# A fused attention and feed-forward kernel on one core: all steps in another order, with the transposing loads of v and the loads of q and k issued further ahead

## The chip, the core and the metric

The kernel runs on one core of a Trainium2 chip, alone. The metric is its time on the device in microseconds; the profile is one execution taken by the hardware profiler.

## What is computed

```python
def _attn_ref(q, k, v, tau):                         # q, k, v: (4, 6080, 256) float32, tau = 1.0
    qn = q / (np.linalg.norm(q, axis=1, keepdims=True) + 1e-06)
    kn = k / (np.linalg.norm(k, axis=1, keepdims=True) + 1e-06)
    s = kn.transpose(0, 2, 1) @ qn / tau             # (4, 256, 256)
    s = s - s.max(-1, keepdims=True)
    a = np.exp(s)
    a /= a.sum(-1, keepdims=True) + 1e-09
    return v @ a

def _moe_ref(x, w_in, w_out):                        # x: (24320, 256), w_in: (256, 2048), w_out: (2048, 256)
    h = x @ w_in
    c = np.sqrt(2.0 / np.pi)
    g = 0.5 * h * (1.0 + np.tanh(c * (h + 0.044715 * h * h * h)))
    return g @ w_out                                 # (24320, 256) float32

def reference(...):
    return _moe_ref(_attn_ref(q, k, v, tau).reshape(24320, 256), w_in, w_out)
```

The attention is across channels: its matrix of scores is 256 x 256 for each of the four batches, summed over 6,080 rows.

## The kernel before, in words

**The work of a batch.** The matrix of scores of a batch is built from q and k, which come in chunks (batch 0 in six, the others in eight chunks of six or so rows for each partition). A chunk's `lq` and `lk` load q and k with a cast to bf16 (L98, in buffers of five per tensor); `qsq` and `ksq` square them (L192, L194), `row0` to `row5` add to the matrix on TensorE (L253, two matmuls each), `f1`, `f2`, `f3` fold the squares on VectorE, `sp` sums them on TensorE, and `sa` (L240) adds them to the norms of the batch. When all chunks are in, a chain of small steps makes the softmax: `gc`, `pow` (a power on POOL, L375), `kf` (VectorE, L381), `kr`, `krp`, `S0`, `S1`, `th0`, `th1`, `dn`, `rc0` to `rc3`, `eT`, `rsum`, `rs`. Since `v @ a @ w_in` is `v @ (a @ w_in)`, the batch's matrix is multiplied into w_in: `aw0` to `aw7` on TensorE (L454), `ac0` to `ac7` copy the result out, `SW0` to `SW2` make sums of it.

**The work of a block.** The output is done in 48 blocks of 512 rows, 12 for each batch, the last of a batch with 448. A block needs v transposed. `lv` casts the block of v to bf16 into a buffer in DRAM (L152, five of them), and `lt` loads it from there with a transposing DMA (L162) into `vT`, of which there are four buffers; the first three blocks of batch 0 are transposed by TensorE instead. The block's first product gives 16 pieces of the hidden layer in eight pairs. A pair is done plainly by `g0` to `g7` (four matmuls of 512 columns, L521) with its GELU in `G0` to `G7` on ScalarE (L531), or two pairs together as a set `w0`, `w1`, `w2`, with seven small products in place of eight: `m1` to `m7` (two matmuls of 256 columns each, L602), copies `cq` and `y5` on ScalarE, sums `ap` (L623) and `ax` (L626) on VectorE, and GELUs `Gq`, `Gr`, `Gx` on ScalarE (L628, L633, L636). The sets need differences of vT, which `vs` makes on VectorE (`sums_v`, L558, L560, L561). Blocks have two or three sets (set 0 alone in block 2, none in blocks 0 and 1). The second product is done in the same way with seven in place of eight: `T1a`, `T2`, `T3`, `T4` on VectorE (L692, L704, L706, L708), `M1A` to `M7B` on TensorE (L736, four matmuls of 256 columns each), `cq`, `y5`, `ap`, `ax`, and four 32 x 32 transposes `c11`, `c12`, `c21`, `c22` on VectorE (L761). The fourth of them issues the block's store, four DMAs on SP's queue (L828).

**The order.** Up to the first product of block 0 the kernel issues its instructions in the order of the code. From there on the order is written out by hand in `ORDER`, a list of 48 strings. String n holds steps in the order in which they are issued, each with the number of the block that it belongs to as a distance from n: in string 3, `M3A-2` is a step of block 1 and `lt+2` the load for block 5. For the steps on q and k, number n stands for chunk n % 12 - 1 of batch n // 12 + 1. There is no scheduler behind it: every engine and every queue gets its instructions in this order and goes through them one by one; semaphores hold an instruction until its inputs are there and its buffer is free. Stores and transposing loads share SP's queue. `lv`, `lq` and `lk` are issued by POOL, whose queue has `pow` in it too, and each waits, as a gate, for the last matmul of the first product (`g` or `m`) ahead of it in the list:

```python
GATE[0] = mm                                   # in mm1 (g); small (m) does the same
...
elif what == "lt":
    load_vt(n)                                 # nc.sync.dma_start_transpose, no gate
elif what == "lv":
    cast_v(n, GATE[0])
elif what in ("lq", "lk"):
    load_one(b, c, "qk".index(what[1]), GATE[0])
```

## Time and profile before

| | |
|---|---|
| time, median of 3 runs | 710.44 us (710.06 to 710.8) |
| the profiled execution's own time | 711.88 us |
| its span, first to last instruction | 709.7 us |
| mean granted TensorE clock | 0.995 |
| busy: TensorE, its weight loads | 681.2 us (96%), 543.6 us (77%) |
| busy: VectorE, ScalarE, POOL | 637.1 us (90%), 625.7 us (88%), 73.4 us (10%) |
| HBM read, written | 78.91 MB, 36.57 MB |

Times in the profile are counted from the first instruction. PE is TensorE, PEld its weight loads, DVE VectorE, ACT ScalarE, POOL GpSimd, SP the engine that issues stores and transposing loads; a q behind a name is that engine's sequencer or queue. A matmul's end is modelled, and a few per cent of the matmuls have no record, so a busy TensorE is not one at its peak. Where an engine was idle ahead of an instruction, the idle time and what ended it stand in brackets, or behind the arrow. The granted clock is the share of the full TensorE clock. The first 38 us are the start (first chunks of q and k, softmax of batch 0); the part that `ORDER` writes out runs from there to the end.

### The profile page before, as it was taken

The numbers are of one execution on the slowest core, as the hardware profiler recorded it, in microseconds if no ns is written. First come the engines' busy times: TensorE is split into PE (matmuls) and PEld (weight loads), VectorE is DVE, ScalarE is ACT, GpSimd is POOL, SyncE is SP. The second block draws the span as 40 slices with busy tenths as digits, with TensorE's granted clock in tenths as the row PEclk, the third lists the DMA queues.
The fourth block names the chain that finished last, engine by engine and source line by source line (L and its number), as shares of the span: only waits on it lengthen the run. The fifth ranks groups of instructions, "written<-read, shape, count | busy, mean of one in ns | idle before, by whom it ended". The sixth has DMA issues, their size and how long they took to land.

```text
span 709.7 us, 14649 instructions
## 1 busy us (share of the span) xinstructions
PE 681.2 (96%) x5634; PEld 543.6 (77%) x5699; DVE 637.1 (90%) x1121; ACT 625.7 (88%) x947; POOL 73.4 (10%) x135
## 2 busy tenths in 40 slices
PE   3999899999999999999999999989999999999996
...
GB/s 242 207 261 198 91 138 127 82 127 197 115 108 91 86 91 141 108 147 133 106 94 115 98 107 116 110 70 86 39 98 90 101 74 57 78 90 59 60 61 56
DMA packets 161462, 79.08 MB, mean 111 GB/s; under 512 B 148448, under 2 KB 152160, under 8 KB 160672
## 3 DMA queue, kind: packets, MB, share of 16 engines
...
HBM read 78.91 MB, written 36.57 MB: 163 GB/s over the span
## 4 chain that ended last, share of the span: by engine, by line
PE 77%; DMA 8%; ACT 8%; DVE 3%; issue 2%; SPq 0%; POOL 0%; DVEq 0%; POOLq 0%; ACTq 0%
PE rp L736 34%; PE h L521 14%; PE rb L602 13%; PE qp L602 10%; PE G L253 4%; DMA vT<-vb 3%; DMA last<-in_k_dram 2%; PE awp L454 2%; ACT g L628 1%; DMA qk_f<-in_q_dram 1%; ACT yw L621 1%; ACT qp L618 1%; DMA win_bf<-in_moe_w_in_dram 1%; ACT g L531 1%; DMA t<-in_k_dram 1%
## 5 line engine op out<-in xcount | busy, mean ns | idle before, releaser
L736 PEld LDWEIGHTS <-wcomb 128*128 128x128 bf16 x2688 | 261.6, 98 | 50.5 <-issue 8.3
L736 PE MATMUL rp<-t,wcomb 128*128 128x256 bf16 (+1 forms) x1504 | 206.6, 272 | 2.2 <-DVE c L752 1.8
L736 PE MATMUL rp<-g,wcomb 128*128 128x256 bf16 (+1 forms) x1128 | 160.5, 272 | 0.5 <-ACT rp L782 0.3
L531 ACT ACTIVATE g<-h 128x1024 bf16<-128x1024 f32 (+1 forms) x136 | 137.2, 1016 | 15.3 <-PE h L521 13.3
L628 ACT ACTIVATE g<-qp 128x1024 bf16<-128x1024 f32 (+1 forms) x124 | 124.7, 1013 | 11.6 <-PE qp L602 9.2
L602 PEld LDWEIGHTS <-sw 128*128 128x128 bf16 x992 | 95.9, 98 | 30.7 <-issue 7.7
L521 PE MATMUL h<-vT,aw 128*128 128x512 bf16 (+1 forms) x403 | 111.9, 376 | 3.0
L623 DVE TENSOR_TENSOR qp<-rb,yw 128x512 f32<-128x512 f32 (+1 forms) x124 | 85.1, 687 | 11.2 <-PE rb L602 6.1
L602 PE MATMUL rb<-tv,sw 128*128 128x256 bf16 (+1 forms) x496 | 93.6, 273 | 0.9 <-ACT qp L618 0.3
L626 DVE TENSOR_TENSOR xw<-rb,yw 128x512 f32<-128x512 f32 (+1 forms) x124 | 83.4, 674 | 6.9 <-PE rb L602 5.0
L602 PEld LDWEIGHTS <-aw 128*128 128x128 bf16 x744 | 72.8, 98 | 13.8
L521 PEld LDWEIGHTS <-aw 128*128 128x128 bf16 x544 | 52.7, 98 | 38.9 <-DVE aw L362 0.6
L636 ACT ACTIVATE g<-xw 128x512 bf16<-128x512 f32 (+1 forms) x124 | 77.3, 625 | 4.4 <-DVE xw L626 4.1
L618 ACT ACTIVATE qp<-rb 128x512 f32<-128x512 f32 (+1 forms) x124 | 71.9, 582 | 5.6 <-PE qp L602 1.5
L633 ACT ACTIVATE g<-rb 128x512 bf16<-128x512 f32 (+1 forms) x124 | 72.7, 593 | 4.1 <-PE rb L602 4.0
L621 ACT ACTIVATE yw<-qp 128x512 f32<-128x512 f32 (+1 forms) x124 | 73.0, 594 | 3.5 <-PE qp L602 1.9
L192 ACT ACTIVATE sq<-t 128x1536 bf16<-128x1536 bf16 (+4 forms) x49 | 64.6, 1335 | 6.0 <-DMA t<-in_q_dram 6.0
L761 DVE STREAM_TRANSPOSE ot<-rp 128x256 f32<-128x256 f32 (+1 forms) x141 | 59.1, 434 | 8.3 <-PE rp L736 6.1
L253 PE MATMUL G<-t 128*128 128x256 bf16 (+1 forms) x352 | 61.0, 280 | 0.1
L708 DVE TENSOR_TENSOR t<-t,g 128x2048 bf16<-128x2048 bf16 (+2 forms) x49 | 57.9, 1184 | 2.0 <-ACT g L633 0.8
L706 DVE TENSOR_TENSOR t<-g 128x2048 bf16<-128x2048 bf16 (+2 forms) x49 | 57.7, 1180 | 0.1
L692 DVE TENSOR_TENSOR t<-g 128x2048 bf16<-128x2048 bf16 (+1 forms) x48 | 57.5, 1198 | 0.1
...
## 6 DMA issues: line engine op xcount, KB each, us to landing
...
vb<-in_v_dram POOLq DMA_DIRECT2D x41, 256.0 KB, 4.6
...
```

Source lines behind the costliest of these rows:

```text
L253: nc.tensor.matmul(G[b][:, jc, :], lhsT=qt[:np_, r, jc * 128 : jc * 128 + 128], rhs=kt[:np_, r, :], start=first and jc == 0, stop=jc == 1, ...
L521: mm = nc.tensor.matmul(hp[:, u, :cols], lhsT=AW[b][:, cc, fc * 128 : fc * 128 + 128], rhs=vt_tiles[n][:, cc, :cols], start=cc == 0, stop= ...
L531: nc.scalar.activation(gs(n)[:, 2 * p : 2 * p + 2, :cols], HP.pop((n, p))[:, :, :cols], AF.Gelu_apprx_tanh)
L602: GATE[0] = nc.tensor.matmul(acc[:, u * hc : u * hc + hc], lhsT=lhs[:, u * 128 : u * 128 + 128], rhs=rhs, start=m in (1, 5) and u == 0, st ...
L618: nc.scalar.activation(qp(n, i)[:, 0, :c], RB[n, i][:, :c], AF.Copy)
L621: nc.scalar.activation(YW[n, i][:, :c], qp(n, i)[:, 1, :c], AF.Copy)
L623: nc.vector.tensor_add(qp(n, i)[:, 1, :c], RB[n, i][:, :c], YW[n, i][:, :c])
L626: nc.vector.tensor_add(XW[n, i][:, :c], RB[n, i][:, :c], YW.pop((n, i))[:, :c])
L628: nc.scalar.activation(gs(n)[:, 2 * pa : 2 * pa + 2, :c].rearrange("p u (t x) -> p t u x", t=2), QP.pop((n, i))[:, :, :c].rearrange("p t ( ...
L633: nc.scalar.activation(gs(n)[:, 2 * pb : 2 * pb + 2, :hc], two(RB.pop((n, i))[:, :c]), AF.Gelu_apprx_tanh)
L636: nc.scalar.activation(gs(n)[:, 2 * pb : 2 * pb + 2, hc:c], two(XW.pop((n, i))[:, :c]), AF.Gelu_apprx_tanh)
L736: nc.tensor.matmul(ACCS[n, acc][:, :hc], lhsT=wcomb[:, w, fc, :], rhs=x, start=first and k == 0, stop=k == 3, skip_group_check=True)
```

## The change

All 48 strings of `ORDER` are replaced, and nothing else in the code. Both lists hold the same 3,897 steps of the same blocks, so the kernel issues the same instructions, with the same shapes, tiles and buffers. What differs is the order on each engine and queue, and with it the matmul on which a gated load waits. Most steps move by a few places; loads and casts move by up to several blocks. By the TensorE steps ahead of them in the list, 26 of the 45 `lt`, 24 of the 48 `lq` and `lk` and 21 of the 45 `lv` stand earlier than before, the others later. Below are the strings of which the text speaks, before and after.

```diff
 ORDER = [
@@ strings 0 to 3 @@
-    """g0 lv+3 aw2 lv+4 ac2 aw4 ac4 lq+1 g1 lk+1 G1 G0 aw3 lq+2 ac3 aw5 ac5 aw6 g3 G3 aw7 g2 ac6 G2
-    ac7 g7 G7 pA11 SW0 vtp vtc0 g6 G6 lv+5 vtc1 pS3 g5 vtq G5 g4 G4 pA12 M1B""",
-    """g3 G3 T1a-1 pF0-1 pS1-1 M1A-1 pF1-1 pS2-1 g0 G0 M5A-1 T2-1 T4-1 M5B-1 y5-1 cq-1 g1 G1 lq+2
-    g2 M2B-1 lq+4 M6B-1 g7 pNA-1 G2 M6A-1 vtr0-1 M2A-1 G7 lk+1 qsq g6 G6 pS4-1 g5 c11-1 ap-1
-    M3B-1 T3-1 vtr1-1 vs+1 G5 M7A-1 M7B-1 ax-1 g4 G4 lk+2""",
-    """w0m1 T1a-1 ksq-1 w0m5 M3A-2 w0cq w0y5 M4A-2 M4B-2 c21-2 g0 G0 c12-2 c22-2 lq+2 w0m6 w0ap
-    M1A-1 M5A-1 M5B-1 ksq lt+1 lv+5 T2-1 f1-1 M1B-1 g3 w0m7 w0ax w0m2 w0m3 y5-1 cq-1 M6B-1 M6A-1
-    G3 g7 T4-1 w0Gq w0m4 G7 w0Gr M2B-1 T3-1 M2A-1 c11-1 ap-1 w0Gx g4 vs+1 G4 g5 T1a G5 M3B-1
-    lk+2 M7A-1 SW2-2 g6 G6 row4-1 SW1-2""",
-    """w0m1 w0m5 w0cq M3A-2 w0y5 f2-2 row3-1 M7B-2 ax-2 w0m6 w0ap g3 ksq M4A-2 lt+1 M4B-2 G3 c21-2
-    row5-2 w0m7 c12-2 c22-2 g0 w0ax qsq M1A-1 G0 w0Gx f3-2 M1B-1 T2-1 T4-1 M5B-1 w0m4 w0Gr M5A-1
-    y5-1 cq-1 T3-1 w1m1 w0m2 w0m3 w0Gq T1a sp-2 sa-2 row1-2 w1m5 w1cq w1y5 M6A-1 M6B-1 g7 G7
-    w1m6 w1ap M2B-1 M2A-1 c11-1 row0-2 row5+1 lt+2 ap-1 qsq-1 f1-1 f2-1 g4 M3B-1 G4 M7B-1 M7A-1
-    ax-1 qsq+1 row5-1 w1m7 w1ax w1m2 w1m3 c22-1 M4B-1 lk+2 M3A-1 M4A-1 row3-2 w1Gx f3-1 sp-1
-    w1Gq vs+1 sa-1""",
+    """g0 lv+3 aw2 ac2 aw5 ac5 aw4 g1 G0 ac4 aw3 ac3 aw7 aw6 ac6 G1 ac7 g3 G3 pS3 g2 G2 pA11 g7 G7
+    vtp vtc0 lv+4 g6 G6 M1B lq+1 g5 G5 lq+2 g4 G4 vtc1 SW1 T1a pF0 M1A pA12 vtq""",
+    """g3 pS1-1 G3 pF1-1 pS2-1 g0 G0 M5A-1 M5B-1 lk g1 g2 lk+1 T2-1 vtr1-1 y5-1 cq-1 M2B-1 M6A-1
+    lq+2 G1 T4-1 g7 lt+2 G2 lt+3 M6B-1 vtr0-1 T1a G7 g6 G6 pNA-1 lq+3 M2A-1 pS4-1 c11-1 ap-1 g5""",
+    """w0m1 g4-1 G5-1 G4-1 M3B-2 T3-2 M7A-2 M7B-2 SW0-2 lk+1 M3A-2 vs w0m5 w0cq ax-2 g5 c12-2 w0y5
+    row1-1 G5 T2-1 w0m6 row3-1 M4A-2 w0ap M4B-2 g0 c21-2 w0m7 M1A-1 M5A-1 qsq-1 ksq w0ax c22-2
+    G0 SW2-2 w0m2 w0m3 w0Gq M1B-1 M5B-1 T3-1 y5-1 cq-1 w0Gx row4-1 w0m4 g3 G3 lk+2 ksq-1 g6 G6
+    M2A-1 M6B-1 f1-1 T4-1 g7 w0Gr lv+3 lv+5 lt+3 G7 M2B-1 M6A-1 g4 G4""",
+    """w0m1 c11-2 ap-2 M3A-2 vs w0m5 M3B-2 c12-2 w0cq T1a-1 g3 w0y5 G3 w0m6 M7A-2 M7B-2 w1m1 w0ap
+    qsq-1 g0 lq+2 G0 ax-2 M4A-2 M4B-2 T2-1 c21-2 c22-2 w0m7 lv+3 w0ax w0m2 w0m3 w0Gq w1m5 w1cq
+    M1B-1 M5A-1 M1A-1 M5B-1 row4-1 w0m4 row0-2 w1m6 f2-2 row5-2 y5-1 cq-1 M6B-1 M2A-1 T3-1 qsq
+    M6A-1 f3-2 w0Gx M2B-1 T4-1 g7 w0Gr vs+1 w1y5 sp-2 row2-2 c11-1 G7 ap-1 M7A-1 lk+3 M7B-1 w1ap
+    w1m2 w1m3 f1-1 w1m7 ax-1 lk+2 g4 qsq+1 f2-1 f3-1 lq+3 M4A-1 G4 M4B-1 sa-2 w1ax T1a sp-1 sa-1
+    w1Gx lt+3 M3A-1 M3B-1 lv+5 c22-1""",
 ...
@@ strings 9 to 10 @@
-    """w0m5 f2-1 w0m1 w0cq w0y5 g0 lt+2 M4A-2 w0m6 row4-1 lq+5 lv+3 G0 w1Gx-1 w0ap M4B-2 c21-2 w1m1
-    w1m5 w1cq w0m7 w1y5 w0ax w0Gx row5-2 w0m3 M1B-1 f3-1 c22-2 w1m6 w1ap gc w0m4 w0Gr M1A-1
-    M5B-1 M5A-1 y5-1 T2-1 lk+6 cq-1 w1m2 w1m3 vs+1 w0m2 w1Gq w0Gq sp-1 sa-1 w1m7 w1ax T3-1 pow
-    M6A-1 M6B-1 M2B-1 w2m1 M2A-1 c11-1 ap-1 w2m5 w1Gx g3 w2y5 w2cq w1m4 w1Gr G3 M3B-1 T4-1 w2m6
-    M3A-1 w2ap kf kr M7A-1 M7B-1 ax-1 w2m3 w2m2 c12-1 w2Gq w2m7 w2ax krp S1+1 th1+1 M4A-1 S0+1
-    th0+1 M4B-1""",
-    """w0m5 c22-2 c21-2 w0m1 w0cq g0 w0m6 T1a-1 M1A-1 M1B-1 w0y5 w0ap lt+2 dn rc1 rc0 G0 w2Gx-1
-    T2-1 M5A-1 M5B-1 y5-1 w0m3 w0m2 g3 w0Gq w2m4-1 w2Gr-1 w0m7 g4 rc2 w1m1 cq-1 M2B-1 rc3 w0ax
-    M6B-1 G3 G4 lq+5 w1m5 M6A-1 lt+3 w1cq eT w1y5 M2A-1 c11-1 w0Gx w1m6 w0m4 w0Gr g7 G7 ap-1
-    M3A-1 w1ap w1m7 w1m2 w1m3 w1Gq M3B-1 T3-1 vs+1 lq+7 rsum+1 rs+1 w1ax T4-1 M7A-1 M7B-1 ax-1
-    w1Gx aw0+1 ac0+1""",
+    """w0m1 w0m5 w1ax-1 w1m4-1 w0cq w0y5 M3A-2 M4A-2 w0m6 T1a-1 f1-1 M4B-2 g0 lk+5 f2-1 w1Gr-1 w0ap
+    w0m3 f3-1 w1Gx-1 c21-2 w0m7 w1m1 c12-2 w0ax G0 T2-1 T4-1 w0m2 w0Gq M1A-1 M1B-1 w1m5 w1cq
+    w0m4 row4-2 w0Gr w1y5 M5A-1 M5B-1 y5-1 cq-1 w1m6 sp-1 w2m5 sa-1 w2y5 w0Gx w1ap T3-1 row2-2
+    row1-2 w2m1 w2cq pow M6A-1 w1m2 w1m3 w1Gq kf w1m7 w1ax gc lq+5 lv+5 M6B-1 M2B-1 c22-2 kr
+    w2m6 w2ap M2A-1 w1Gx g3 G3 c11-1 ap-1 w2m7 w2ax w2Gx krp S0+1 S1+1 th1+1 M7A-1 M7B-1 w2m3
+    w1m4 w1Gr w2m2 w2Gq ax-1 M4B-1 M4A-1 vs+1 c22-1""",
+    """w0m5 w0m1 w0cq w0y5 T1a-1 M3B-2 M3A-2 th0 dn w0m6 c12-2 c21-2 w0ap w2m4-1 g0 T2-1 M1A-1 G0
+    rc1 M1B-1 rc2 w0m3 w0m2 w0Gq w0m7 lq+3 w2Gr-1 T4-1 w0ax M5A-1 T3-1 M5B-1 y5-1 cq-1 rc0 g3 G3
+    g4 G4 w1m1 M2A-1 w1m5 w1cq M6A-1 w1y5 M6B-1 w0m4 w0Gr w0Gx w1m6 w1ap M2B-1 g7 lt+2 lt+3
+    c11-1 ap-1""",
 ...
@@ strings 23 to 24 @@
-    """g3 G3 M7B-2 rc0-1 g0-1 G0-1 ax-2 g7-1 G7-1 c12-2 eT-1 w1ax-1 M4A-2 rsum rs w0m1 T1a-1 w0m5
-    w0cq w0y5 M4B-2 c21-2 w1m4-1 w1Gx-1 aw0 ac0 w0m6 w1Gr-1 g0 lk+5 G0 M1B-1 aw1 ac1 w0ap w0m7
-    w0m3 T2-1 w0m2 w0Gq lv+4 w1m1 w1m5 w1y5 w1cq lt+2 aw2 w0ax w0Gx ac2 T3-1 M1A-1 M5A-1 M5B-1
-    y5-1 cq-1 w1m6 w1ap w0m4 w2m5 w0Gr aw3 ac3 M2B-1 M6A-1 w2m1 w1m7 M6B-1 lv+6 SW0 qsq+2 M2A-1
-    w1ax aw4 w1m3 w2y5 w2cq w2m6 w1Gx lt+3 ac4 w1m2 w1Gq w1m4 w1Gr c11-1 ap-1 M3A-1 M7A-1 w2ap
-    T4-1 M7B-1 aw5 M3B-1 vs+1 w2m3 ac5 c22-2 w2m2 w2Gq""",
-    """w0m5 w0m1 w0cq lv+6 aw6-1 ac6-1 w0y5 w2m7-1 ax-2 M4A-2 M4B-2 T1a-1 w0m6 g3 G3 w2ax-1 w2m4-1
-    c21-2 c12-2 aw7-1 w0ap w0m7 M1B-1 f1+1 ac7-1 w2Gx-1 w0m3 w0m2 g0 w0Gq M5B-1 SW1-1 T2-1 M5A-1
-    G0 M1A-1 w2Gr-1 g7 w0ax vs+1 y5-1 w1m1 cq-1 w1m5 w1cq M6A-1 w1y5 M6B-1 G7 row3+3 w1m6 w0Gx
-    f2+1 w1ap T4-1 w0m4 w0Gr row5+1 M2A-1 M2B-1 lv+4 c11-1 ap-1 w1m3 w1m2 w1Gq g4 T3-1 lt+3 G4
-    row4+2""",
+    """g3 G3 lv+3 g0-1 G0-1 M7A-2 rc0-1 lt+2 M7B-2 g7-1 w0m5 w0Gr-1 G7-1 rc2-1 rc1-1 rc3-1 eT-1
+    ax-2 w1m1 rsum rs lq+6 w0m1 M4A-2 w0cq lv+5 T1a-1 aw0 ac0 M4B-2 w0m6 w0y5 w0ap w1Gx-1 lk+4
+    g0 G0 c12-2 aw1 c21-2 T2-1 ac1 w0m3 w0m2 w0Gq w0m7 M1A-1 M5A-1 aw2 w0ax lv+6 ac2 T3-1 w1m5
+    w1y5 w1cq lt+3 M1B-1 M5B-1 lv+4 aw3 ac3 w2m5 w1m6 w1ap y5-1 cq-1 w0Gx w0m4 w0Gr M2B-1 M6B-1
+    w2y5 w2m1 M6A-1 M2A-1 w2cq lq+5 T1a w2m6 qsq+2 aw4 ac4 w1m3 w1m2 w1m7 w1Gq c11-1 ap-1 M3A-1
+    M7B-1 w2ap w2m3 lv+8 w2m7 w1ax w1m4 M7A-1 w1Gx lk+5 w1Gr w2m2 w2Gq vs+1 aw5 ac5 M3B-1""",
+    """w0m1 SW0-1 w0m5 c22-3 T4-2 w0cq w0y5 ax-2 g3 aw6-1 ac6-1 w2ax-1 w0m6 M4B-2 w0ap M4A-2 f1+1
+    c21-2 aw7-1 c12-2 w0m3 w0m2 ac7-1 w2Gx-1 T2-1 SW1-1 w2m4-1 G3 w0m7 g0 M1A-1 w0Gq w2Gr-1 w0ax
+    T4-1 G0 M1B-1 M5A-1 M5B-1 y5-1 cq-1 w1m1 w1m5 w1cq g7 w1y5 M2B-1 G7 w1m6 w1ap w0m4 w0Gr vs+1
+    M6A-1 M2A-1 M6B-1 c11-1 ap-1 T3-1 w1m3 w1m2 w0Gx w1Gq g4 G4 w1m7 M3A-1""",
 ...
@@ strings 28 to 30 @@
-    """w0m5 w1m4-1 row0-2 row1-1 w1Gr-1 M3B-2 w0m1 w0y5 lk+4 w0cq row2-1 T4-2 row5 T1a-1 M3A-2
-    w2Gr-1 w0m6 w0ap w1Gx-1 M7A-2 w1m1 M7B-2 f3-1 ax-2 ksq+1 w0m7 w0ax w0m3 w0m2 w0Gq g0 G0
-    M4B-2 M4A-2 w2m5 w2y5 lk+3 w0m4 T2-1 w0Gr g3 c21-2 G3 c12-2 row4 row4-1 w2m1 w2cq T4-1 M1B-1
-    M5B-1 w0Gx w1m5 w1y5 T3-1 w2m6 w2ap M1A-1 w1cq M5A-1 lq+2 c22-2 w2m7 w2ax w2m3 w1m6 w1ap
-    y5-1 cq-1 w2m2 M2A-1 M2B-1 c11-1 w2Gx w1m7 w1ax w2Gq lq+3 w1m3 w1m2 w1Gq row4+1 M6B-1 w1m4
-    w1Gr M6A-1 w2m4 vs+1""",
-    """w0m5 w0y5 w0m1 w0cq ap-2 M3A-2 M7A-2 M7B-2 w2Gr-1 w1Gx-1 vs+1 w0m6 w0ap qsq-1 M3B-2 c12-2 g0
-    G0 w0m7 w0m2 w0m3 ax-2 lk+1 w0ax w0Gq T1a-1 M4A-2 M4B-2 c21-2 w0m4 g3 w2m5 w0Gx w0Gr M1A-1
-    M1B-1 M5A-1 M5B-1 qsq T2-1 T3-1 sp-2 sa-2 c22-2 row3+2 row5+2 row0+2 lt+2 w2m1 y5-1 cq-1
-    M6A-1 M2B-1 f1-1 f2-1 f3-1 w2y5 M2A-1 lq+3 w2cq w2m6 w2ap G3 qsq+2 M6B-1 w1m5 c11-1 ap-1
-    w1m1 lv+5 w1cq row2+2 w2m3 w2m2 w2Gq w2m7 w2ax T4-1 M7A-1 M3B-1 w1m6 w1y5 M3A-1 w1ap w2m4""",
-    """g0 w2Gx-1 M7B-2 w2Gr-1 ax-2 G0 w1m7-1 w1ax-1 w1m3-1 w1m2-1 w1Gq-1 sp-2 sa-2 M4B-2 T1a-1
-    M4A-2 w1Gx-1 w1m4-1 g3 w1Gr-1 G3 w0m5 row0 row5 w0y5 w0m1 w0cq c12-2 ksq+1 c21-2 M1A-1 M5A-1
-    w1m5 c22-2 M1B-1 w0m6 T2-1 M5B-1 row0-1 vs+1 row2-2 w0ap w1m1 w0m3 w0m2 T4-1 w0m7 y5-1 cq-1
-    w1cq M6B-1 w1y5 w1m6 row0+2 w0Gq row4+2 M2A-1 w0ax w0Gx w0m4 w1ap w1m7 w0Gr w1m3 w1m2 w1Gq
-    g7 G7 f1-1 w1ax w1m4 w1Gr""",
+    """w0m5 w0y5 row0-1 c11-2 ap-2 T1a-1 row3 M3B-2 w0m1 w0cq f2-1 g0 lq+3 w0m6 M3A-2 row5+1 w2Gr-1
+    M7A-2 ksq+1 G0 w0ap w0m7 w0ax M7B-2 ax-2 w0m3 row2+1 w0m2 w0Gq w0m4 w0Gr M4A-2 M4B-2 T3-1 g3
+    w2m1 c12-2 w0Gx G3 w1m1 w2m5 w2y5 c21-2 c22-2 vs+1 M1B-1 M5B-1 w1m5 M5A-1 row0+1 T2-1 w2cq
+    w2m6 M1A-1 row1-1 w1y5 w1cq w1m6 row4 y5-1 cq-1 w2ap w2m7 w1ap w2m3 qsq w2ax w2Gx M6B-1
+    M6A-1 w1m3 w1m2 w1Gq T4-1 w1m7 w1ax w2m2 w2Gq M2A-1 M2B-1 c11-1 ap-1 w2m4 w1m4 w1Gr row0+2
+    T1a row2""",
+    """w0m5 M3B-2 w0y5 vs+1 w0m1 lt+2 w0cq lv+4 f3-2 M7B-2 w1Gx-1 M3A-2 w0m6 M7A-2 qsq g0 G0 w0ap
+    ax-2 w0m7 w0ax w0m2 M4A-2 w2Gr-1 M4B-2 c12-2 w0m3 w0Gq w0m4 w0Gx w0Gr c21-2 c22-2 g3 G3
+    M1A-1 T2-1 T4-1 M1B-1 lq+3 M5A-1 M5B-1 w1m1 sp-2 sa-2 row4+2 w2m5 w1m5 w2m1 row0+2 y5-1 cq-1
+    M2A-1 M6A-1 T3-1 w2y5 w2cq f1-1 w2m6 w2ap w1cq w1y5 M6B-1 f2-1 qsq+2 lv+6 M2B-1 c11-1 ksq+2
+    row5+2 row3+1 ap-1 w2m7 w2ax w1m6 w1ap w2Gx w2m3 w2m2 w2Gq f3-1 M3B-1 lv+3 M7A-1 M7B-1 w1m7
+    ax-1 w1ax T1a w2m4 w2Gr w1m3 w1m2 w1Gq M4B-1 M4A-1 M3A-1 c12-1 w1m4 w1Gr sp-1 sa-1 lk+3
+    c21-1 f1""",
+    """g3 w0m5 w0m1 M1A-1 M5B-1 w1Gx-1 T3-1 G3 w0y5 w1m1 g0 w0cq w0m6 M1B-1 G0 M5A-1 y5-1 cq-1 T2-1
+    row2+1 w1m5 w1cq w0ap w1y5 w0m7 w0m3 vs+1 w0ax w0Gx w0m2 M2A-1 w1m6 w1ap c22-2 M6B-1 M6A-1
+    f2-1 M2B-1 c11-1 ap-1 w0Gq lt+2 lt+3 w0m4 w0Gr w1m3 w1m2 f3-1 w1Gq g7 G7 M3A-1 T1a w1m7 w1ax
+    ksq""",
 ...
@@ string 33 @@
-    """w0m5 w1m4-1 w1Gx-1 G7-1 sp-1 sa-1 w1Gr-1 g0 row3-3 G0 T3-1 gc M4B-2 M4A-2 c21-2 w1m1 c12-2
-    w0y5 w0m1 w0cq T2-1 g3 G3 pow kf kr M1A-1 M1B-1 w0m6 w0ap M5B-1 M5A-1 w1m5 y5-1 cq-1 vs+1
-    w0m7 w0ax w0m2 w0m3 M6A-1 M6B-1 T4-1 lt+2 w1cq w1m6 w1y5 M2A-1 w0Gq w1ap c22-2 w0m4 M2B-1
-    c11-1 ap-1 w0Gx krp S1+1 S0+1 lt+4 w0Gr T1a w1m3 w1m2 w1Gq g4 G4 M7B-1""",
+    """g0 f1-1 c12-2 w1Gq-1 f2-1 f3-1 M7B-2 sa-2 sp-1 G0 M7A-2 T1a-1 row4-1 w1m1 row1-3 sa-1 ax-2
+    vs+1 pow kf w0m1 w0m5 lt+3 M4B-2 M4A-2 c21-2 w1Gx-1 gc g3 T3-1 w0y5 w0cq w0m6 w0ap M1A-1
+    M5B-1 M5A-1 M1B-1 kr lv+4 G3 T2-1 krp S0+1 y5-1 w1m5 cq-1 w0m7 w1cq w1y5 T4-1 th0+1 w0m2
+    w0m3 w0Gq w0ax M2B-1 M2A-1 w1m6 M6B-1 w0Gx M6A-1 w0m4 w0Gr w1ap w1m7 c22-2 S1+1 th1+1 w1m3
+    w1m2 w1Gq g4 G4 c11-1 ap-1 M3B-1 M3A-1 M7B-1 dn+1""",
 ...
@@ string 47 @@
-    """w0m5 M4A-2 c22-2 M4B-2 w1Gx-1 w2Gq-1 T1a-1 w0y5 w0m1 w0cq M3B-2 c12-2 c21-2 w2Gx-1 g3 T3-1
-    G3 w1m4-1 w2m4-1 w1Gr-1 w0m6 M1B-1 w0ap w2Gr-1 M1A-1 M5B-1 M5A-1 w0m2 y5-1 cq-1 w1m5 T2-1
-    T4-1 w1m1 w1cq w1y5 w0m3 w0Gq w0m7 M6B-1 M6A-1 w0ax w0Gx w1m6 M2A-1 M2B-1 w1ap c11-1 ap-1
-    w2m5 w2m1 w1m7 w1ax w2y5 w1m3 w1m2 w2cq w1Gq w0m4 M7A-1 w2m6 w2ap w1m4 w0Gr M7B-1 g0 G0 w2m7
-    ax-1 M3A-1 M4A-1 M4B-1 w2ax w2Gx T1a w1Gr M3B-1 c12-1 c21-1 c22-1 w1Gx T2b w2m3 w2m2 w2Gq
-    M5A T2a M5B y5 T3a M1B M1A w2m4 cq T3b M3A M6B w2Gr M6A y6 M3B M7A a12 c12 M7B ax c22 sA T4b
-    M4B M2B T4a M2A c11a c11 M4A c21 sB""",
+    """w0m1 w0m5 ax-2 M4A-2 w0y5 w0cq w1Gx-1 T1a-1 M4B-2 w2ax-1 w2Gx-1 c22-2 M3B-2 c12-2 w1m4-1
+    w1Gr-1 w2m4-1 c21-2 w2Gr-1 w0m6 w0ap g3 G3 M1B-1 M1A-1 M5B-1 M5A-1 y5-1 cq-1 w0m7 w1m5 w1m1
+    T2-1 w0m2 w0m3 M6A-1 w1cq w1y5 T4-1 M6B-1 w1m6 M2B-1 w0ax w0Gq w0Gx T3-1 M2A-1 w1ap w2m5
+    w2y5 w2m1 w2cq w0m4 w1m3 w1m2 w1Gq c11-1 ap-1 w1m7 M7A-1 w1ax w2m6 w1Gx M7B-1 w2ap ax-1 w0Gr
+    w1m4 g0 w2m7 M3A-1 w2ax M4A-1 G0 M4B-1 w2Gx T1a M3B-1 w2m3 w2m2 w1Gr w2Gq c21-1 c12-1 c22-1
+    M5A M5B y5 M1A T2b M1B cq T2a w2m4 T3a w2Gr T3b M3A M6B M6A T4b y6 M3B a12 c12 M7A M7B ax
+    c22 T4a M4A M4B c21 M2A M2B sA c11a c11 sB""",
 ]
```

367 lines of the change are left out of this document (184 added, 183 removed).

## The prediction

> **What bounds the kernel now.** I read the page's slices first, then the stretches (busy time of each engine, granted clock, DMA share), then the chain of work that ended last, and last the timeline at the places where the stretches fall off.
>
> ```profile
> span 709.7 us, 14649 instructions
> ...
> PE   3999899999999999999999999989999999999996
> ```
>
> After the start TensorE is in the nineties throughout, but for an 8 in the fifth and one in the 27th slice. In the stretches the columns are PE, PEld, DVE, ACT and POOL busy, granted clock, DMA share, GB/s.
>
> ```profile
> 37.85:705.70 667.85, 655.08 (x5384) 523.15 (x5449) 619.29 (x1091) 608.88 (x930) 56.87 (x104) 0.99 0.61 105
> 40.00:50.00 10.00, 9.95 (x62) 5.16 (x61) 9.30 (x17) 8.06 (x9) 2.37 (x5) 1.00 1.16 278
> 50.00:60.00 10.00, 9.91 (x66) 6.34 (x65) 9.52 (x14) 9.97 (x12) 1.61 (x3) 1.00 1.06 210
> 75.00:100.00 25.00, 23.14 (x193) 18.16 (x193) 23.79 (x49) 20.42 (x29) 1.53 (x3) 1.00 0.57 104
> 100.00:150.00 50.00, 49.62 (x434) 41.08 (x437) 46.74 (x81) 47.72 (x71) 6.80 (x13) 1.00 0.63 107
> 300.00:350.00 50.00, 49.34 (x418) 39.76 (x421) 47.69 (x88) 48.05 (x74) 6.70 (x12) 1.00 0.83 136
> 450.00:460.00 10.00, 9.95 (x88) 8.11 (x87) 8.65 (x15) 9.87 (x14) 0.81 (x2) 1.00 1.12 135
> 464.10:470.90 6.80, 5.97 (x29) 4.11 (x29) 4.73 (x7) 2.25 (x3) 0.00 (x0) 0.50 0.64 120
> ```
>
> An ordinary stretch (100 to 150, 300 to 350) leaves TensorE 0.4 to 0.7 us idle in 50; VectorE and ScalarE follow at 47 and 48. So TensorE is the bound, and the other two have too little slack to make up a stop. Two stretches are not ordinary: 1.86 us idle in 75 to 100, and a clock of 0.50 from 464.1 to 470.9. The chain at the first:
>
> ```profile
> 65.06 0.87 SPq L828
> ...
> 66.04 7.01 DMA vT<-vb
> 73.06 0.02 issue
> 73.08 0.44 DVE tv L558
> ```
>
> The timeline behind it, with the idle time ahead of an instruction and what ended it in brackets:
>
> ```profile
> 77.88 1.03 PE L736 MATMUL rp<-t,wcomb 128*128 128x256 bf16 x8 [1.75 <-DVE c L752]
> ```
>
> The chain at the second, and its timeline:
>
> ```profile
> 450.99 12.11 DMA vT<-vb
> ```
>
> ```profile
> 463.19 0.43 DVE L558 TENSOR_TENSOR tv<-vT 128x512 bf16<-128x512 bf16 x1 [3.33 <-DMA vT<-vb]
> ...
> 464.93 0.58 PE L602 MATMUL qp<-vT,sw 128*128 128x256 bf16 x2 [3.04 <-DVE qp L623]
> ```
>
> Both times a transposing load of v lands at the moment at which VectorE wants it for `sums_v` (L558). VectorE's queue stands behind that instruction, its other results come late, and TensorE stops: 1.75 us before 77.88, 3.04 before 464.93. After the second stop the clock is 0.50 for 6.8 us, which costs 6.8 x 0.5 = 3.4 more. **The two places hold 1.75 + 3.04 + 3.4 = 8.2 us.** The list of waits, over the whole span, has no third (us in total, times, longest):
>
> ```profile
> DVE tv L558 <- DMA vT<-vb: 5.5, 2, 3.3
> ```
>
> **What the change does to the loads of v.** Both orders have the same 3,897 steps, so the sum consists of waits alone. To compare, I lay both orders on TensorE's work, with each step at what TensorE takes for it back to back in the chain:
>
> ```profile
> 449.94 0.44 PE rp L736 x4
> 450.38 0.22 PE rb L602 x2
> ```
>
> ```profile
> 78.91 0.22 PE G L253 x2
> 79.13 0.22 PE rb L602 x2
> 79.35 0.86 PE h L521 x4
> ```
>
> A `g` is 0.86, an `M` 0.44, a small product or a `row` 0.22 (0.863, 0.436 and 0.218 unrounded), an `aw`, two of the four matmuls of a `g`, 0.43. There are 136, 672, 868, 144 and 30 of them; with 7/8 of it in the four short blocks that is 642.6 us with the odd small steps. Counted from 37.85, a load of v can be issued when three things are over: what is ahead of it on SP's queue (a store waits there for its block's fourth transpose, then takes 2.2), the last use of the buffer that it takes over (there are four), and its own cast (6 us after the matmul on which that is gated).
>
> ```profile
> 80.33 2.19 SPq L828 DMA_DIRECT2D out_dram<-ot  x4
> ```
>
> ```profile
> vb<-in_v_dram POOLq DMA_DIRECT2D x41, 256.0 KB, 4.6
> ```
>
> A load's lead is the TensorE work from there to its first use. In the order before, the shortest come out as 4.7 (block 3), 4.8 (14), 8.6 (42), 10.7 (31) and 11.1 (28). The rows above have 4.9 for block 3 (66.04 to 73.08, less its wait, the 5.5 - 3.3 = 2.2 of the list) and 8.9 for block 31 (450.99 to 463.19, less 3.33), so the method is good to some 2 us. Against them, the landing of all 45 loads:
>
> ```profile
> DMA to landing us min/median/max: 3.0/4.2/12.1
> ```
>
> In the order after, the shortest leads are 16.2 (block 32), 17.1 (27), 17.3 (43) and 17.5 (40). Block 3's load moves from string 2, behind the store of block 0, to string 1 with no store ahead of it: its lead goes from 4.7 to 28.2, block 31's from 10.7 to 25.8. Seventeen of the 45 get a shorter lead, but none goes under 16.2, which is 4 us more than the longest landing. So both stops go: -8.2.
>
> **The loads of q and k** go from a shortest lead of 6.5 (q of step 7) to 9.8 (q of step 17); half of the 48 stand later in the order than before, so it is the short ones that grow. Times to landing of those issued from 40 to 44.2 us, then of those from 53 to 61:
>
> ```profile
> DMA to landing us min/median/max: 12.6/13.0/13.5
> ```
>
> ```profile
> DMA to landing us min/median/max: 4.4/6.8/7.3
> ```
>
> The one at risk is k of step 1: its gate lets it go at 50.5, and `row1-1` in string 2 wants it at 61.7, a lead of 11.2. It lies between the two groups, nearer to the later. Taken at 8 to 9 it costs nothing; at 13.5 it costs 2.3.
>
> **What else moves.** `kf` on VectorE needs `pow` on POOL, which needs `sa` on VectorE:
>
> ```profile
> 504.74 0.15 DVE L240 TENSOR_TENSOR sv<-sv,ss 128x4 f32<-128x4 f32 x1
> ...
> 504.97 1.95 POOL L375 TENSOR_TENSOR rt<-sv,halves 128x4 f32<-128x4 f32 x1 [6.04 <-DVE sv L240]
> ```
>
> ```profile
> L375 POOL TENSOR_TENSOR rt<-sv,halves x3: 1027/1049/1952, 170.9 to 505.0; 128x4 f32<-128x4 f32 x3
> ```
>
> Before, 3 to 4.3 us of VectorE's steps lie between `sa` and `kf` in all three batches. After, it is 1.8 in the first, 4.9 in the second and 1.3 (one add and one `sums_v`) in the third. `pow` is over 0.23 + 1.05 or 0.23 + 1.95 us after `sa` starts, so VectorE stands 0 to 0.4 in the first and 0 to 0.9 in the third, with its whole queue behind `kf`. I take 0.3 for both, as two of the three durations are near the short one.
>
> The small waits are left. 667.85 less 642.6 is 25.3; without the 8.2 there remain 17 us, 0.3 or so for each of the 48 blocks. For twelve kinds of pairs (VectorE or ScalarE makes something, a step of TensorE reads it) I counted how often less TensorE work lies between the two than the making takes: 321 of 1,158 pairs before, 293 after. In proportion that would be 1.5 us fewer; VectorE's work is a little more bunched, though (below). I take 0, with a bound of 2 us down and 3 up. The end, where T4 is done in halves with products behind it, keeps one stop in either order: 0, within the same bounds.
>
> **Sum.** The profiled execution took 711.88 (its span and 2.18 around it); less 8.2, plus 0.3, that is 704.0. The median of the timed runs, 710.44, lies 1.44 under it: 710.44 - 7.9 = **702.5 us**. That difference also says that the 6.4 us at 462 are in the timed runs: an execution that had them alone would lie at least that far above the median.
>
> The price of the second stop rests on the clock. The Trainium skill ("TensorE: Matmul & The Clock Gate", section "HAM oscillation — how this bites in real kernels") has it that idle gaps of over about 3.4 us are to be avoided. Here a gap of 3.04 us had half the clock for 6.8 us behind it: the trace is harsher than the rule. By the rule alone that stop would be worth 3.04, and the sum would be 705.9.
>
> **The rivals.**
> *The early loads collide at the start (0.10).* Two transposing loads now run from about 50 us, beside q and k of the first chunks, where the DMA share is 1.16 and 1.06: nothing is to spare. If k of step 1 lands only 13.5 us after its issue, TensorE stands 2.3 us at `row1-1`: 704.8. If the transposing loads add some 3 us each, the stop goes past the 3.04 us at which the clock fell and is worth about 6.4: 708.9. Against it, fewer loads are queued ahead of it. Before, five are issued by 44 us:
>
> ```profile
> 39.18 1.05 POOL L152 DMA_DIRECT2D vb<-in_v_dram  x2 [1.96 <-PE h L521]
> 40.22 0.58 POOL L98 DMA_DIRECT2D t<-in_q_dram  x1
> 41.23 0.54 POOL L98 DMA_DIRECT2D t<-in_k_dram  x1 [0.43 <-PE h L521]
> 43.55 0.53 POOL L98 DMA_DIRECT2D t<-in_q_dram  x1 [1.78 <-DMA wst<-in_moe_w_out_dram]
> ```
>
> After, it is one by 44 and four by 47. The skill has the reason in general ("DMA: Bandwidth & Descriptors", section "Issuing engines are not separate DMA queues"): DMAs of all queues run on the same 16 engines and interleave, so an earlier issue brings no bandwidth.
> *The 12.1 us landing is the profiled execution's own (0.04).* Then only 1.75 goes: 710.44 - 1.75 + 0.3 = 709.0. Against it stands the 1.44 above.
> *The change does not do what it says (0.02),* because SP's queue or the buffers hold the loads as before: 710.4. Against it, the leads above have queue and buffers in them.
> *VectorE's work is bunched and stops TensorE (0.17), slower.* With its steps scaled to what VectorE is busy (619.29), each free to start where it stands in the order, they queue up 6.3 us deep in string 24 after (5.8 in string 10, 5.0 in string 23), where a batch's softmax and its products with w_in come on top; before, those three have 2.7, 3.8 and 3.1. If TensorE then stands as it did at 462, each place costs 6.4. From the second such stop it decides: 702.5 + 2 x 6.4 = 715.3. One alone leaves the kernel faster (708.9). Against it: before has 5.4 in string 1 and 5.3 in string 20, and the stretches that hold them (50 to 60, 300 to 350) do not fall off.
>
> **How the numbers follow.** Forecast 0.67, rivals 0.10, 0.04, 0.02 and 0.17. The range goes down to 700.5 by the 2 us of the small waits, and up to 710.5, which leaves out the slower rival alone. A measurement of this kernel can tell about 0.2% (1.4 us) from no change: faster by more are the forecast and the collision (0.77), within it are the landing of one execution and the idle change (0.06), slower is the bunching (0.17).
>
> **What would show it.** Right: no wait of L558 for vT, no stretch with a clock under 1.00, no 8 in TensorE's slices after the start; at most 1 us of waiting at `kf` near 500. Wrong: a stop of TensorE over 1 us in strings 10 or 23 to 25 that VectorE ends, a wait for `in_k_dram` or `in_q_dram` near 62 us, or another stretch at half the clock.

## The result and the profile after

| | before | after |
|---|---|---|
| median of the timed runs, us | 710.25 (6 runs, 709.07 to 712.25) | 699.41 (6 runs, 699.12 to 705.56) |
| profiled execution, us (span) | 711.88 (709.7) | 705.56 (703.8) |

The ratio is 0.986, with a 95% interval of 0.9825 to 0.9895: the kernel after is faster by 10.8 us. The forecast was 702.5 with a range from 700.5, so the direction was right and the gain was larger than the range allowed for. The profiled execution is the slowest of the six of after; the other five lie 5.3 us and more under it, and its profile shows why. The page, span and TensorE's slices:

```profile
span 703.8 us, 14646 instructions
...
PE   3997999999999999999999999999999999999996
```

The two 8s of before, in the fifth slice and near 462 us, are gone; there is a new 7 in the fourth slice. The stretches (columns as before: PE, PEld, DVE, ACT and POOL busy, granted clock, DMA share, GB/s):

```profile
60.00:65.00 5.00, 2.84 (x23) 2.02 (x21) 3.76 (x11) 4.36 (x6) 0.53 (x1) 1.00 1.03 47
65.00:70.00 5.00, 3.03 (x15) 2.16 (x15) 0.70 (x1) 0.57 (x1) 0.00 (x0) 0.67 1.04 201
75.00:100.00 25.00, 24.84 (x198) 18.96 (x200) 22.87 (x41) 21.54 (x27) 4.70 (x9) 1.00 0.92 161
100.00:150.00 50.00, 49.79 (x437) 41.82 (x440) 47.66 (x83) 48.07 (x75) 7.40 (x15) 1.00 0.78 128
300.00:350.00 50.00, 49.56 (x417) 39.96 (x421) 47.16 (x88) 48.20 (x74) 5.61 (x8) 1.00 0.61 106
460.00:470.00 10.00, 9.93 (x80) 7.65 (x79) 9.35 (x17) 9.51 (x16) 0.50 (x1) 1.00 0.58 93
```

From 75 to 100 TensorE is idle for 0.16 us instead of 1.86, and from 460 to 470 it runs at full clock: both stops of before are gone, and the list of waits has no entry of L558 for vT any more. What is new lies from 60 to 70. The chain of waits, the list of waits and the timeline there:

```profile
52.29 14.64 DMA t<-in_k_dram
66.93 0.04 issue
66.97 0.59 PE G L253 x2
```

```profile
PE G L253 <- DMA t<-in_k_dram: 4.5, 2, 4.1
```

```profile
66.97 0.59 PE L253 MATMUL G<-t 128*128 128x256 bf16 x2 [4.13 <-DMA t<-in_k_dram]
```

k of step 1, the load that the prediction named as the one at risk, took 14.64 us to land, TensorE stood for 4.13 us at `row1-1`, and the clock fell to half behind it. That is the first rival, in this one execution, and one of the signs of being wrong that the prediction names (a wait for `in_k_dram` near 62 us, with half the clock behind it).

To see the rest I lay both orders on TensorE's work as the prediction does, and now subtract that work from the start that each block's first step has in the trace. What is left is the time that TensorE has lost so far, from block 0 on. For the kernels of this document, in us (the experiments follow below):

| lost by block | 2 | 4 | 23 | 30 | 31 | 47 |
|---|---|---|---|---|---|---|
| before | 0.6 | 2.9 | 8.5 | 11.1 | 17.2 | 22.3 |
| after, first profile | 1.2 | 7.3 | 11.2 | 12.2 | 12.4 | 16.6 |
| after, third profile (e15) | 1.0 | 1.2 | 5.2 | 6.2 | 6.4 | 10.6 |
| two loads and k moved (e7) | 0.7 | 0.8 | 6.4 | 9.1 | 9.3 | 14.5 |
| order of before, leads of after (e2) | 0.9 | 1.0 | 6.5 | 9.1 | 9.5 | 14.5 |
| after, k of step 1 earlier (e4) | 0.9 | 1.2 | 5.1 | 6.1 | 6.3 | 10.4 |
| first half of before, second of after (e10) | 0.5 | 0.5 | 6.0 | 7.6 | 7.8 | 11.7 |
| e2 with 27 rows as fill (e12) | 0.7 | 0.8 | 6.3 | 10.4 | 11.0 | 16.0 |

Before loses 2.3 at block 3 and 6.1 at block 30, which are the two stops (8.4), and 13.9 in small waits. After loses 5.9 at block 2, which is the late load, and 10.7 in small waits. So the small waits, which the prediction took to stay, sum to 3.2 us less.

### The profile page after: what moved, and what is told of

Its sections match the earlier page's. It is cut to its first block, busy times and chain, and to the rows that moved or that the text cites. A ratio compares the mean times of both kernels' runs of the same rounds, so it can differ in the third digit from the quotient of the medians.

```text
span 703.8 us, 14646 instructions
## 1 busy us (share of the span) xinstructions
PE 676.3 (96%) x5635; PEld 543.6 (77%) x5699; DVE 636.4 (90%) x1121; ACT 625.2 (89%) x947; POOL 74.2 (11%) x135
## 4 chain that ended last, share of the span: by engine, by line
PE 75%; ACT 9%; DMA 7%; issue 4%; DVE 4%; POOL 0%; DVEq 0%; POOLq 0%; ACTq 0%
PE rp L736 34%; PE rb L602 13%; PE h L521 12%; PE qp L602 10%; PE G L253 5%; DMA t<-in_k_dram 5%; ACT g L628 2%; ACT yw L621 1%; DMA t<-in_q_dram 1%; ACT qp L618 1%; ACT g L531 1%; PE awp L454 1%; DMA out_dram<-ot 1%; ACT sq L192 1%; ACT g L633 1%
## 5 line engine op out<-in xcount | busy, mean ns | idle before, releaser
L253 PE MATMUL G<-t 128*128 128x256 bf16 x352 | 59.7, 278 | 4.5 <-DMA t<-in_k_dram 4.5
L704 DVE TENSOR_TENSOR t<-g,t 128x2048 bf16<-128x2048 bf16 (+2 forms) x49 | 57.4, 1173 | 0.5 <-ACT g L636 0.2
```

The lines of the kernel that those rows point to most:

```text
L253: nc.tensor.matmul(G[b][:, jc, :], lhsT=qt[:np_, r, jc * 128 : jc * 128 + 128], rhs=kt[:np_, r, :], start=first and jc == 0, stop=jc == 1, ...
```

## The experiments

The theory to test (A): the gain is made of two parts, the two stops behind late transposing loads of v, and small waits that hang on the order of the computing steps. Against it stood that the two loads are the whole gain, that the stop at 462 us belonged to the profiled execution, or that the order of the computing steps alone did it. Kernels that are compared with each other in the first four experiments ran on one chip, beside the kernel before (710.19, 17 runs). e5 to e8, e9 to e12 and e13 to e15 ran on three other chips; the kernel before took 710.49, 710.20 and 711.53 there.

**e1: two loads moved in the kernel before.**

```diff
 # string 1
-M3B-1 T3-1 vtr1-1 vs+1
+M3B-1 T3-1 vtr1-1 lt+2 vs+1
 # string 2
-ksq lt+1 lv+5
+ksq lv+5
 # string 28
-M5A-1 lq+2 c22-2 w2m7
+M5A-1 lq+2 c22-2 lt+3 w2m7
 # string 29
-row0+2 lt+2 w2m1
+row0+2 w2m1
```

> The kernel before, with two transposing loads of v moved and nothing else: that of block 3 from string 2 to string 1 (behind `vtr1-1`, with no store ahead of it), that of block 31 from string 29 to string 28 (behind `c22-2`, ahead of the store of block 27). Theory A (the two stops behind late loads are worth 8.2 us in the timed runs, and the rest of the gain, some 3 us, are small waits that hang on the order of the computing steps): 710.25 - 8.2 = 702.0, no wait of L558 for vT at blocks 3 and 31. Rival B (the two loads are the whole of it): 699.4. Rival C (the stop and the half clock at 462 us belong to the profiled execution of before): 708.5, as only the 1.75 us of block 3 go.

Measured: 715.66 us, ratio 1.0075 (1.0053 to 1.0098). Slower than before, which no theory had. The stop at 462 is gone, but at 67 us there is a larger one than either of before. The list of waits, TensorE's timeline, and the stretch:

```profile
DVE sq L194 <- DMA t<-in_k_dram: 14.7, 3, 9.3
```

```profile
75.73 0.61 PE L736 MATMUL rp<-t,wcomb 128*128 128x256 bf16 x2 [9.00 <-DVE t L704]
```

```profile
70.00:80.00 10.00, 4.26 (x17) 2.43 (x18) 5.83 (x6) 0.63 (x1) 0.00 (x0) 0.52 1.07 193
```

VectorE waits 9.3 us for k of step 2 (`ksq` on it, L194), its queue stands behind that, and TensorE stops for 9.00 us, with half the clock after it. Between 51 and 61 us, the loads issued and their median times to landing:

```profile
t<-in_q_dram POOLq DMA_DIRECT2D x2, 384.0 KB, 16.8
t<-in_k_dram POOLq DMA_DIRECT2D x2, 384.0 KB, 16.1
vT<-vb SPq DMA_TRANSPOSE x1, 19.4
```

In the kernel before, the loads of q and k of these microseconds took 4.4 to 7.3 us. The transposing load of block 3, now issued at 49.7, takes 19.4, and the loads of q and k that run beside it are slow as well. What moved was one load; what came late was another one.

**e2: all loads as far ahead as after, the computing steps as before.** The four kinds of load steps of before's order are put at the lead that they have after (or as far as the ring of buffers allows); all other steps keep their order.

> The computing steps in the order of before, and every load of q, k and v as far ahead of its first use, in TensorE work, as in the order after (or as far as its ring of buffers lets it in this order). Theory A: 702.0, the same as with the two loads alone, as the small waits hang on the computing steps. Rival (the small waits come from loads too, as each landing that falls late holds VectorE a little): 699.4, and the drift of TensorE against its own work falls by 3 us in blocks 4 to 30.

Measured: 703.43 us (703.08 to 704.19), ratio 0.9902 (0.9881 to 0.9922). 6.8 of the 10.8 us come from the loads. In the table it has lost 14.5 at the end, and from block 4 to 30 its small waits grow by 8.1 as in before (8.2): theory A, not the rival. It lies 1.4 over the 702.0 of theory A; the stops are worth less in the timed runs than in the profile of before (e5 and e7 below).

**e3: the computing steps as after, the loads at the leads of before.** The other way about.

> The computing steps in the order of after, and every load as far ahead of its first use as in the order before. Theory A: the loads of blocks 3 and 42 stand 5.6 and 5.4 us of TensorE work ahead of their use, so stops behind L558 come back: 699.4 plus 1.8 to 8.2, that is 701.2 to 707.6, and the sum with the kernel of only the loads moved comes out (702.0 - 710.25 = -8.2 there, -2.6 to -9 here). Rival (the order of the computing steps carries the gain and the leads are nothing): 699.4, with no wait of L558 for vT over 0.5 us.

Measured: 707.74 us (706.74 to 709.76), ratio 0.9968 (0.9954 to 0.9982). The waits for late loads of v are back:

```profile
DVE tv L558 <- DMA vT<-vb: 6.6, 3, 3.6
```

The order alone gives 2.5 us, just outside what theory A allowed (701.2 to 707.6). The late loads are those of blocks 3, 9 and 14, not 3 and 42 as expected. Against e4 (next), TensorE loses 4.2 us more at block 3 and 4.3 at block 9, and nothing at block 14, where VectorE waits 0.7; these 8.5 us are what the times differ by (707.74 - 699.37 = 8.4). The leads are needed for the order to show.

**e4: after, with k of step 1 issued earlier.**

```diff
 # string 0
-vtp vtc0 lv+4 g6 G6 M1B lq+1 g5
+vtp vtc0 lv+4 g6 G6 M1B lq+1 lk+1 g5
 # string 1
-M5B-1 lk g1 g2
+M5B-1 g1 g2
```

> The kernel after, with one load moved: k of step 1 from string 1 to string 0, right behind q of step 1. Theory A (the 5.9 us by which the profiled execution of after lies above the timed runs are the late landing of this load at 67 us, with the half clock behind it, and that comes in some executions only): median 699.3, no execution over 701, and no wait of TensorE for in_k_dram near 63 us in the profile. Rival (the transfers of 56 to 66 us are slow whichever load is first, and the next load in the queue is late instead): executions at 705 stay, and q or k of step 2 holds TensorE or VectorE.

Measured: 699.37 us (698.99 to 700.99), ratio 0.9849 (0.9825 to 0.9873). k of step 1 lands at 55.5, 6.9 us ahead of its use, and TensorE has no wait for it (its one wait for `in_k_dram`, of 0.6 us, lies in the start). Beside e2, on the same chip, this is the order of the computing steps with the loads out of the way: 703.43 - 699.37 = 4.1 us. The profiles say the same:

```profile
span 702.1 us, 14714 instructions
```

```profile
span 697.6 us, 14709 instructions
```

From the start of block 0 (38.1 and 37.7) that is 664.0 against 659.9, 4.1 apart, and the two orders have lost 14.5 and 10.4 by block 47. A stretch of the same length, e2 and then e4:

```profile
100.00:660.00 560.00, 558.12 (x4686) 449.14 (x4685) 526.85 (x931) 526.26 (x815) 45.97 (x84) 1.00 0.60 101
```

```profile
100.00:660.00 560.00, 559.03 (x4724) 453.19 (x4723) 529.84 (x939) 529.17 (x822) 45.81 (x83) 1.00 0.62 100
```

In 560 us the order after gets 38 more matmuls done, at 560/4,724 = 0.119 us each some 4.5 us (neither trace lacks a matmul: both have 5,699, as many as weight loads). The idle column alone (0.9 us apart) doesn't show it: a matmul that waits 0.1 to 0.2 us stays inside a busy stretch, as the ends of matmuls are modelled.

**e5: block 31's load alone.** As e1, without the move of block 3's load.

> The kernel before, with one load moved: the transposing load of block 31 from string 29 to string 28. Theory A (the two moved loads of the first experiment did opposite things: block 31 gained its 6.1 us, block 3's early load made k of step 2 late and cost the rest): 710.2 - 6.1 = 704.1 against executions that have that stop, so a median of 704 to 706, TensorE at full clock at 462. Rival (moving block 31's load gains nothing in the timed runs): 710.

Measured: 705.69 us (705.42 to 707.68), against 710.49 for before on that chip (11 runs, 708.44 to 713.06); ratio 0.9934 (0.9914 to 0.9954). This stop is worth 4.8 us in the timed runs, not the 6.4 of the profile: of the 11 executions of before on that chip, the five with a mean granted clock of 0.999 or more lie at 708.4 to 710.6, the other six (0.995 to 0.997) at 710.1 to 713.1. So the half clock doesn't follow in every execution, and its cost comes in several sizes; of the timed executions only the mean clock is on record, so whether the stop itself varies too is not shown.

**e6: a plain load in the place of block 3's transposing one,** in the kernel of e1.

```diff
-nc.sync.dma_start_transpose(out=vT[:, :, :cols], in_=v_bf.pop(n)[:cols, :])
+if n == 3:
+    nc.sync.dma_start(out=vT.rearrange("p a b -> p (a b)"),
+                      in_=v_bf.pop(n).rearrange("(p r) c -> p (r c)", p=128))
+else:
+    nc.sync.dma_start_transpose(out=vT[:, :, :cols], in_=v_bf.pop(n)[:cols, :])
```

> The kernel with the two moved loads, and for block 3 a plain load of the same 256 KB at the same moment instead of the transposing one (block 3 then computes with v in another arrangement: the transposition of one block is left out). Theory A (the transposing load slows the casts of q and k that run beside it): k of step 2 lands 7 to 9 us after its issue instead of 17.6, no stop at it, 715.7 - 11.6 = 704 or less. Rival (256 KB more at that moment are too much for the DMA engines, in whatever form): k still lands after 15 us or more, and the time stays at 715.

Measured: 704.23 us (703.88 to 704.29). The loads issued between 51 and 61 us:

```profile
t<-in_q_dram POOLq DMA_DIRECT2D x2, 384.0 KB, 7.9
t<-in_k_dram POOLq DMA_DIRECT2D x2, 384.0 KB, 7.0
```

The same bytes from the same queue at the same moment, not transposed, leave q and k at half the time to landing, and the 11 us of e1 are gone. It is the transposing load that slows its neighbours, not its size. What in it does so is open: the plain load went as 144 packets in all, the transposing one as 847 in the ten microseconds from 51 alone, and no run took the transposition and the small packets apart.

**e7: the two loads of e1, and k of step 2 earlier too.**

```diff
 # string 0
-aw3 lq+2 ac3
+aw3 lq+2 lk+2 ac3
 # string 1
-G7 lk+1 qsq
+G7 qsq
```

> The kernel with the two moved loads, and k of step 2 moved too, from string 1 to string 0 behind q of step 2. Theory A (the collision costs only the load that has the shortest lead): k of step 2 lands before 62 us, no stop of TensorE at 70 us, both stops of before are gone: 710.2 - 8.2 = 702.0. Rival (the next cast that stands beside the transposing load, q of step 3 or k of step 3, is late instead): a stop of 2 us or more elsewhere before 110 us, 704 to 716.

Measured: 704.09 us (703.78 to 705.83) against 710.49; ratio 0.9915 (0.9896 to 0.9935). The transposing load is still slow (18.1), and so is k of step 2 (15.3), but that is issued at 44.8 and lands at 60.2, 3.9 ahead of its use by VectorE (L194 at 64.03) and 13.6 ahead of TensorE's. No stop is left, as theory A had it, but the time is 2.1 over its 702.0: both stops are worth 6.4 us together, 4.8 for block 31 (e5) and 1.6 for block 3. It took three moved loads, not two; and the small waits are those of before's order, block by block (14.5 at the end, as in e2).

**e8: rows as fill in the order after.** A `row` needs q and k that have landed and the bank of its batch's matrix, so most of them can stand ahead of any matmul that waits.

```diff
 # string 16, one of 15 such moves
-w0m6 w0ap row3+1 row1
+row1 w0m6 w0ap row3+1
```

> The kernel after with k of step 1 earlier, and 15 `row` products of q and k moved a little forward (0.4 to 7.6 us of TensorE work), each to stand ahead of a matmul that waited 0.08 to 0.24 us in that kernel's trace; the 15 waits sum to 2.25 us. Theory A (the small waits are single matmuls that stand too close behind the step that makes their operand, and hang on the order alone): 2 us less, 697.3, and those 15 waits gone from the trace. Rival (VectorE and ScalarE have too little slack, so a wait that is filled comes back further on): 699.3, and the drift of TensorE is the same at the end.

Measured: 699.45 us (699.21 to 699.53). No gain: the rival. The places that were filled wait less, and the next ones wait more: in e4, 0.20 us are lost from block 27 to 28 and 0.12 from 29 to 30; here it is 0.07 and 0.34. At the end it has lost 10.3 instead of 10.4.

**e9 and e10: half of one order, half of the other.** Strings 0 to 23 of one kernel, the remaining steps in the order of the other.

> Blocks 0 to 23 (strings 0 to 23) in the order after with k of step 1 earlier, strings 24 to 47 with the computing steps in the order of before and the leads of after. Theory A (the small waits belong to each block's own order, whatever comes before it): the drift of TensorE against its work is 5.1 us at block 23 as in the kernel with k earlier, and grows by 8.1 from there as in the kernel with only the leads changed, so 699.4 + 2.8 = 702.1. Rival (they are the sum of a shortage over the whole span, given back or taken up later): 700 or 703.5, as one order or the other has it.

> The other way about: strings 0 to 23 with the computing steps of before and the leads of after, strings 24 to 47 in the order after. Theory A: the drift is 6.45 us at block 23 and grows by 5.3 from there, 699.4 + 1.4 = 700.8. Rival: 699.4 or 703.5.

e10 measured 701.02 us (700.97 to 701.07), 0.2 from what theory A gave, with 6.0 lost at block 23 and 5.7 from there. So the small waits belong to the stretch of the order in which they stand. e9 measured 711.75 us (705.74 to 719.42; ratio 1.0016, 0.9984 to 1.0048), which neither theory had. It lost 4.9 by block 23 and 8.3 in the remaining blocks without one place, as expected, but at that place, behind the seam, q of step 27 is issued with a shorter lead and meets another slow transposing load (block 26's, 20.5 us to landing):

```profile
PE G L253 <- DMA t<-in_q_dram: 5.2, 1, 5.2
```

**e11: the kernel after again.**

> The kernel after once more, unchanged. Theory A (k of step 1 lands so late only in some executions, as its collision with the transposing load of block 4 hangs on fractions of a microsecond): the median is 699.4, and of the executions none to a third lie at 702 to 706. Rival (the profiled execution was alone in it, something of that one execution): all within 699 to 700.5, profile included.

Measured: 701.38 us (699.54 to 709.47), ratio 0.9893 (0.9854 to 0.9932). The median is 2 us over what theory A gave. Of the six executions two lie over 702, one of them beyond its 706, so the late landing was not that one execution's alone; in the slowest, the profiled one, k of step 1 took 18.2 us:

```profile
70.34 0.58 PE L253 MATMUL G<-t 128*128 128x256 bf16 x2 [7.67 <-DMA t<-in_k_dram]
```

**e12: rows as fill in the order of before** (the kernel of e2, 27 moves as in e8).

> The kernel with the computing steps of before and the leads of after, and 27 `row` products moved a little forward, each to stand ahead of a matmul that waited 0.08 us or more in that kernel's trace; the 27 waits sum to 4.0 us. Theory A (a small wait is one matmul too close behind the step that makes its operand; the order after merely has fewer of them): 703.4 - 4.0 = 699.4. Rival (as in the first such experiment, the waits come back in other places, since VectorE and ScalarE stand no further ahead than before): 703.3.

Measured: 705.27 us (705.14 to 705.35), slower than e2. Of the 4.0 us nothing came in: 0.59 lost from block 19 to 20 in e2 became 0.17, and 0.08 from 20 to 21 became 0.50. One of the moved rows, the first of its batch's matrix, came ahead of the copy (L467) that its bank waits for, and waits itself, which is most of the 1.8 us that are lost against e2:

```profile
373.76 0.38 PE L253 MATMUL G<-t 128*128 128x256 bf16 x2 [1.49 <-DVE aw L467]
```

**e13 to e15: what makes k of step 1 late after.** e13 is the kernel after with the plain load of e6 for block 4 in place of block 3; e14 is e4 again; e15 is the kernel after again, all on one chip (before there: 711.53, 9 runs).

> The kernel after, with a plain load of the same 256 KB for block 4 instead of the transposing one, at the same moment (the transposition of one block is left out). Theory A (the transposing load of block 4 slows the casts beside it, and with them k of step 1): k of step 1 lands 7 to 9 us after its issue instead of 14.6 and 18.2, TensorE does not stop for it, no execution over 700.5, median 699.3. Rival (the transposing load of block 3 or the number of loads does it): landings of 14 us and executions at 702 to 709 stay.

> The kernel after with k of step 1 issued earlier, once more. Theory A: 699.4, all executions within 698.9 to 701, no wait of TensorE for in_k_dram at step 1. Rival (lucky before): some executions at 702 to 710, as in the kernel after beside it.

> The kernel after, unchanged, on the same chip as the two above. Theory A: a median of 699.4 to 701.4 and some executions at 702 to 710. Rival: all within 699 to 700.5.

Measured: e13 699.52 us (699.25 to 700.49), e14 699.88 (699.33 to 700.58), e15 699.85 (699.6 to 701.47). The time to landing of the loads of k issued between 51 and 61 us, in after (first profile), e15 and e13:

```profile
t<-in_k_dram POOLq DMA_DIRECT2D x3, 384.0 KB, 14.8
```

```profile
t<-in_k_dram POOLq DMA_DIRECT2D x3, 384.0 KB, 8.7
```

```profile
t<-in_k_dram POOLq DMA_DIRECT2D x3, 384.0 KB, 7.3
```

And the stretch from 59 to 62 us in the same three, DMA share and GB/s being the last two columns:

```profile
59.00:62.00 3.00, 3.00 (x25) 2.24 (x23) 2.90 (x10) 2.46 (x3) 0.53 (x1) 1.00 1.66 60
```

```profile
59.00:62.00 3.00, 3.00 (x24) 2.25 (x23) 2.90 (x9) 2.39 (x4) 0.53 (x1) 1.00 1.11 213
```

```profile
59.00:62.00 3.00, 2.82 (x23) 2.00 (x22) 2.90 (x9) 2.05 (x4) 0.53 (x1) 1.00 1.09 213
```

The bad execution shows the DMA engines fully busy and moving 60 GB/s; in the good one and without the transposition it is 213. The kernel after itself was good this time (k of step 1 took 8.6, all four executions under 701.5, which fits neither theory of e15), so e13 shows that it goes well without the transposing load of block 4, but its four executions alone don't show that the bad ones are ended by that; e6 shows that for block 3. Of the 16 executions of the kernel after, 3 lie over 702 (703.56, 705.56, 709.47) and 6 over 701; of the 9 with k earlier (e4, e14) none lies over 701. That version has the same median; 3 of 16 against 0 of 9 could still be chance, and what speaks for it is the lead, as k lands 6.8 to 6.9 us ahead of its use (e14, e4). None was faster by more than can be measured.

## Why the prediction was right and where it failed

- **What bounds the kernel, and the two stops (-8.2):** the mechanism was right, the size too large. Both go when the loads have the leads of after (e2, e7), and from profile to profile the size holds: 22.3 - 14.5 = 7.8 lost us. In the timed runs it is 6.4 (e7) to 6.8 (e2). In the trace, the half clock from 464.10 to 470.90 sets in while TensorE still stands (the stop ends at 464.93), so 0.83 us of it lie inside the 3.04 and cost nothing more; the table has 6.1 at block 30 in place of 6.4, and 2.3 at block 3 in place of 1.75, together 8.4. The step that was off is the passage to the median: the 1.44 between the profiled execution and the median of before was kept for the kernel after, but part of it seems to have been the second stop itself, whose cost has several sizes (e5); for e2 the same difference is 704.19 - 703.43 = 0.8.
- **The small waits (0, with a bound of 2 down and 3 up):** this is the step that failed. They fell by 4.1 us (e2 to e4), which alone puts the time under the range. The count of pairs pointed the right way (321 to 293) and its proportion gave 1.5; I then took 0 because VectorE's work is more bunched, and drew the bound too tight. VectorE alone was the wrong place to look. If each matmul's start is compared with the start of the one before it plus that one's own time, and what is over (0.03 us and more) is put down to the engine that ended the wait, the waits that ScalarE ended fall from 8.3 us in e2 to 5.4 in e4, those that VectorE ended only from 5.6 to 4.9. One kind of place can be followed through both traces: from the last of a block's M1 and M5 to the first of its M2 and M6, with the copy `cq` on ScalarE between. Where some 4 products of 0.22 (up to 4.5) lie between, the first matmul behind waits 0.165 us on average in either order; with 5 it is 0.06 in e2 and 0.03 in e4, with 6 or more at most 0.06 on average. e2 has 13 such places with 4, e4 has 6; summed over the blocks it is 3.7 against 1.6 us, half of the 4.1. The count looked at the maker and the reader alone; this way goes from TensorE to ScalarE and back. That the fewer close places are the reason for the smaller sum is argued from the traces, not tested.
- **What sets the sum of the small waits is not settled.** It belongs to the computing order and not to the loads (e2 and e7 agree block by block), and to the stretch where it stands (e10); but single waits that were filled came back within a block or two (e8, e12). So it is not each matmul's distance alone. That VectorE and ScalarE set the pace over a few blocks would fit (the rows of e2 and e4 above have both 94 to 95% busy), but no run took work off them.
- **k of step 1 (0, if it lands in 8 to 9; rival of 0.10):** its lead is 10.4 in e15 (issued at 52.11, used at 62.50) where the prediction had 11.2. It lands in 8.6 there, and in 14.6 and 18.2 in the two other profiles of after, at 5.9 and 10 us lost. The rival's mechanism is shown for block 3's load (e1, e6); for block 4's, which runs beside k of step 1 here, it is only likely (e13). The rival's times of 704.8 and 708.9 lie among the executions of 703.56 to 709.47 by luck: they stand on a 702.5 that was 3.1 too high, and its prices, 2.3 and 6.4, were too small against 5.9 and 10. It comes in 3 of 16 executions, so it doesn't set the median. What was wrong was the row that it was weighed by: the landings of 4.4 to 7.3 us were measured where no transposing load ran beside them.
- **"4 us more than the longest landing":** the landing of 12.1 was not the longest there is. Block 26's load took 21.1 in the first profile of after, and block 4's 17.0. That they cost nothing themselves was luck: the first is issued 33 us ahead of its use, while the shortest lead in e15 is 15.0 (block 32).
- **`kf` behind `pow` (+0.3):** 0. In the third batch `pow` took 1.04, and L381 follows on VectorE with no idle time ahead of it:

```profile
499.63 1.04 POOL L375 TENSOR_TENSOR rt<-sv,halves 128x4 f32<-128x4 f32 x1 [30.58 <-DVE sv L240]
...
500.78 0.16 DVE L381 TENSOR_SCALAR rt<-rt 128x4 f32<-128x4 f32 x1
```

- **The slower rival (VectorE bunched in strings 10, 23, 24):** nothing. In e15 TensorE loses 0.03 over string 10, 0.25 over 23 and 0.06 over 24.
- **The sum again,** with what the runs showed: 710.2 - 6.8 (loads, e2) - 4.1 (order, e4) = 699.3, measured 699.4. This is no check of its own, as the two terms were measured one behind the other and lead to e4's median (699.37); what it shows is that the kernel after has the same median with k of step 1 where it is. Against the terms of the forecast it is 1.4 less for the stops, 0.3 less for `kf` and 4.1 more for the small waits: 702.5 + 1.4 - 0.3 - 4.1 = 699.5. The error in the stops hid a part of the other.
